# Asking for the weights down one tile at a time in a woven transformer block

## The chip, the cores and the metric

One core of a Trainium2 chip runs the whole kernel. The metric is the time of one execution on the device, in microseconds (us); smaller is better. Engines: PE is TensorE (matmul), PEld its weight loads, ACT ScalarE, DVE VectorE, POOL GpSimd. SP is the sync engine, whose queue (SPq) issues nearly all transfers, in the order in which the program lists them: a request that must wait holds back those behind it.

## What is computed

A transformer block in float32 on 2048 rows of width 512: attention with 32 heads of 16 that share one key and one value head, then a gated feed-forward with 1792 inner columns.

```python
def _A_ref(x, wq, wk, wv, wo):
    q = (x @ wq).reshape(B, S, H, Dh).transpose(0, 2, 1, 3)     # H = 32, Dh = 16
    k, v = x @ wk, x @ wv
    scores = jnp.einsum("bhqd,bkd->bhqk", q, k) * (Dh ** -0.5)
    o = jnp.einsum("bhqk,bkd->bhqd", _softmax(scores), v)
    return o.transpose(0, 2, 1, 3).reshape(B, S, H * Dh) @ wo
def _B_ref(x, w_gate, w_up, w_down):
    return (_gelu(x @ w_gate) * (x @ w_up)) @ w_down
h = x + _A_ref(_layernorm(x), A_wq, A_wk, A_wv, A_wo)
h2 = h + _B_ref(_layernorm(h), B_w_gate, B_w_up, B_w_down)      # the result
```

## The kernel before

Each float32 operand of a dense product is split into a high and a low part (hi, lo), and a product is three matmuls: hi by hi, hi by lo and lo by hi. In the early part of the kernel the split weights are written to DRAM scratch: `w1_d` holds 28 tiles of gate and up weights (512 KB each, gate and up in turn for the 14 column blocks f), and `w2_d` 14 blocks of the weights down, loaded two at a time, so 7 tiles of 1 MB.

The rows are worked in four blocks of 512. Attention of a block goes over 8 groups of four heads. A group has 32 score steps: `scores` makes scores (L362), ACT the exponentials (L366), and `weigh` multiplies by the values (L370). At the end of a group its result leaves to DRAM (`acc_d<-oT`, L384), comes back turned (`oc<-acc_d`, L394), and soon the queries for the next group but one step ahead are asked for (`qg<-q_d`, L347).

The dense part of block b (`dense`) is woven into attention of block b + 1, matmul by matmul, by an order that is written out by hand for PE, ACT, SP and DVE. Only the last block's dense part runs by itself at the end (the tail), with whole matmuls and another order (`solo`, L553).

In the woven dense part 36 products are in a list, the plan: gate and up products (pg, pu), each followed at its end by DVE work (`leave_gate`, `leave_up`), and among them the products down (pd) of two of the four runs in `RUNS`; the products down of the last two runs follow behind the weave (`down`, L531). `weave` runs a product as two halves of 12 matmuls, one on rows 0 to 63 of the array and one on rows 64 to 127, with a lag of 6 steps between a product's halves, three banks, and one matmul in each half of the array per step (L854). When a product's second half is issued, its `done` runs: a gate or up product asks for the tile four further on (`next_w1`, `load_w1`, L511; four buffers). Down tiles (`load_w2`, L516) have three buffers.

Numbered in the order of the plan, products 0 to 11 are gate and up products, 12 to 15 products down (first run), 16 to 23 gate and up, 24 to 27 down (second run), 28 to 35 gate and up. Before, the tiles down are asked for a run at a time: both of the first run at the end of product 3, both of the second at the end of product 15, both of the third at the end of product 27, and the single one of the last run at the end of product 33.

Of the kernel before, what the change touches and what calls it, by code (L numbers as in the profile page):

```python
# [10 lines left out]
F32R = mybir.dt.float32r  # L11
# [8 lines left out]
P = 128  # L20
# [6 lines left out]
PB = 5  # L27

W1 = 4

LAG = 6

# [6 lines left out]
RUNS = ((0, 1, 2, 3), (4, 5, 6, 7), (8, 9, 10, 11), (12, 13))  # L39
# [7 lines left out]
def kernel(  # L47
# [15 lines left out]
    S, D = x.shape  # L63
# [6 lines left out]
    TB = T // P  # L70
    DC = D // P
    FC = F // P
# [76 lines left out]
    def run(outer, first):  # L149
# [8 lines left out]
        width = 0  # L158

        def psum1(name):  # L160
            return ps.tile([P, T], F32, tag="d", bufs=width, name=name)
# [170 lines left out]
        if first:  # L332
            set_banks("ps_pro")
            width = 8
# [109 lines left out]
        db = None  # L444
# [63 lines left out]
        def load_w1(b, i):  # L508

            w = db.tile([P, 2, DC, P], F32R, tag="w1", bufs=W1, name=f"w1_{b}_{i}")  # L510
            nc.sync.dma_start(w.bitcast(F32), w1_d[i].bitcast(F32))  # L511
            return w[:, 0], w[:, 1]

        def load_w2(b, j):
            w = db.tile([P, 2, 2, D], F32R, tag="w2", bufs=3, name=f"w2_{b}_{j}")
            nc.sync.dma_start(  # L516
                w.bitcast(F32), w2_d[2 * j : 2 * j + 2].rearrange("f p i d -> p f i d").bitcast(F32)
            )
            return w[:, :, 0], w[:, :, 1]
# [38 lines left out]
        def dense(b, tail=False):  # L558
# [13 lines left out]
            xT_lo = db.tile([P, DC, T], F32R, tag="x2l", bufs=1, name=f"x2l_{b}")  # L572
            w1 = {i: load_w1(b, i) for i in range(W1)}
            if b == 0:
                yield 0
            w2 = {}
# [134 lines left out]
            def next_w1(i):  # L711
                if i + W1 < 2 * FC:
                    w1[i + W1] = load_w1(b, i + W1)

# [53 lines left out]
                    next_w1(2 * f + k)  # L768
                yield CUT

            def up_plan(f, k, then):
                def terms():
                    hi, lo = w1.pop(2 * f + k)
                    return [
                        (w[:, c, :], xt[:, c, :])
                        for c in range(DC)
                        for w, xt in ((hi, xT_hi), (hi, xT_lo), (lo, xT_hi))
                    ]

                def done(bank):  # L780
                    (leave_up if k else leave_gate)(f, bank)
                    next_w1(2 * f + k)
                    if k:
                        then()

                return f"p{'gu'[k]}_{b}_{f}", terms, done

# [11 lines left out]
            def add_down(t, pd):  # L799
                nc.vector.tensor_tensor(hs[t], hs[t], pd, op=ALU.add)  # L800

            def down_plan(fs, t, tw, then):
                def terms():
                    if t == 0:
                        assert not gates and not lazy or all(j // 2 in gs for j in fs)
                        open_gates()
                        while lazy:
                            lazy.pop(0)()
                        tw.extend(w2.pop(f // 2) for f in fs[::2])
                    return down_terms(fs, tw, t)  # L810

                def done(bank):
                    add_down(t, bank)
                    if t == TB - 1:
                        then()

                return f"pd_{b}_{fs[0]}_{t}", terms, done

            def weave(plan):


                live, ends, jobs = [], {}, [None, None]
                step = opened = 0

                def choose(a):
                    nonlocal opened
                    for e in live:
                        if e["half"] != a and not e["both"] and e["at"] and step >= e["at"] + LAG:
                            e["both"] = True
                            return [e, 0]  # L830
                    free = opened < width or ends.get(opened - width, step) + LAG <= step
                    if opened == len(plan) or not free or a == 1 and step < LAG:
                        return None
                    name, terms, done = plan[opened]
                    e = dict(
                        i=opened, half=a, both=False, at=None, terms=terms(),
                        bank=psum1(name), done=done, name=name,
                    )
                    opened += 1
                    live.append(e)  # L840
                    return [e, 0]

                while opened < len(plan) or live:
                    for a in range(2):
                        if jobs[a] is None:
                            jobs[a] = choose(a)
                    for a in range(2):
                        if jobs[a] is None:
                            continue
                        e, i = jobs[a]  # L850
                        lhsT, rhs = e["terms"][i]
                        rows = slice(64 * a, 64 * a + 64)
                        last = i == len(e["terms"]) - 1
                        nc.tensor.matmul(  # L854
                            e["bank"], lhsT[rows], rhs[rows], start=i == 0 and not e["both"],
                            stop=last and e["both"], skip_group_check=True,
                        )
                        jobs[a][1] += 1
                    step += 1
                    for a in range(2):  # L860
                        if jobs[a] is None or jobs[a][1] < len(jobs[a][0]["terms"]):
                            continue
                        e, jobs[a] = jobs[a][0], None
                        if e["both"]:
                            e["done"](e["bank"])
                            live[:] = [z for z in live if z is not e]
                            ends[e["i"]] = step
                        else:

                            mark = sb.tile(  # L870
                                [P, 1], F32, tag="mark", bufs=3, name=f"mark_{e['name']}"
                            )
                            nc.vector.tensor_copy(mark, e["bank"][:, :1])
                            e["at"] = step
                    yield 1
                yield CUT
# [11 lines left out]
                            nc.sync.dma_start(out_t[:, b * TB + t, :], hs[t])  # L888
                    yield CUT

            def fetch_w2(fs):
                for f in fs[::2]:
                    w2[f // 2] = load_w2(b, f // 2)


            plan, prev = [], None
            for fs in RUNS:
                for n, f in enumerate(fs):
                    then = []
                    if fs is RUNS[-1]:  # L900
                        if n == 0:
                            then.append(fs)
                    elif n == 1 and prev is None:
                        then.append(fs)
                    if tail:
                        yield from up(f)
                        for z in then:
                            fetch_w2(z)
                    else:
                        for k in range(2):  # L910
                            plan.append(up_plan(f, k, partial(
                                lambda zs: [fetch_w2(z) for z in zs], then
                            )))
                    if n != 1 or prev is None:
                        continue
                    if tail:
                        yield from down(prev, False)
                        if fs is not RUNS[-1]:
                            fetch_w2(fs)
                    elif fs is not RUNS[-1]:  # L920
                        tw = []
                        plan.extend(
                            down_plan(prev, t, tw, partial(fetch_w2, fs)) for t in range(TB)
                        )
                prev = fs
            if not tail:
                yield from weave(plan)
                yield from down(RUNS[-2], False)
# [19 lines left out]
        def open_gates():  # L948
            while gates:
                gates.pop(0)()  # L950
# [32 lines left out]
        width = 1  # L983
# [5 lines left out]
        n, lead = 0, 2 * PER + sum(SIZES[: LEAD[0]])  # L989
        with tc.manual_schedule(engines={mybir.EngineType.SP, mybir.EngineType.DVE}):  # L990
# [6 lines left out]
            while n < lead:  # L997
                if n == 2 * PER:
# [5 lines left out]
                    db = late.enter_context(tc.tile_pool(name="dense", bufs=1))  # L1004
# [24 lines left out]
        width = 3  # L1029
# [18 lines left out]
        for c in range(LEAD[0], (NB - 1) * NG * len(SIZES)):  # L1048
            b, cb = divmod(c, NG * len(SIZES))
# [4 lines left out]
            if b > 0 and cb == LEAD[b]:  # L1054
                assert work is None
                work, todo = dense(b), list(kinds)
# [58 lines left out]
        tail = dense(NB - 1, True)  # L1115
# [328 lines left out]
```

## Time and profile before

| | us |
|---|---|
| median of three runs | 1472.63 (1469.05 to 1472.9) |
| the profiled execution, its own time | 1469.96 |
| its span, first to last instruction | 1468.3 |
| PE busy | 1418.2 (97%) |
| ACT busy | 1036.0 (71%) |
| DVE busy | 544.7 (37%) |
| POOL busy | 217.8 (15%) |

The early part lasts to about 310 us. The weave of block 0 lies at about 360 to 603 us, that of block 1 at 684 to 944, that of block 2 at 1031 to 1290; the tail takes the last 120 us. In rows of the profile, a name such as `pg<-x2h,w` means a tile pg written from x2h and a weight tile w; `w` stands for tiles of both kinds, and the line (L511 or L516) tells a request for a gate or up tile from one for a tile down. The granted clock is the share of full speed that TensorE had.

### The profile page before, as it was taken

What the parts mean: (1) busy time and instruction counts of PE and PEld (TensorE: products, weight loads), DVE (VectorE), ACT (ScalarE), POOL (GpSimd) and SP (SyncE); (2) the same over time, 40 slices, a digit from 0 to 9 for tenths busy, and PEclk for the clock granted to TensorE, in tenths of its full rate; (3) what the DMA queues carried; (4) which work ended last, traced back from release to release, by engine and by line L of the source; (5) the groups of instructions that cost most, each with busy time, mean ns of one, the idle gap of its engine ahead of it and who ended that gap; (6) DMA issues with size and microseconds to landing.
All of it is one profiled execution on the core that took longest, in us unless ns stands there. A gap on an engine that the chain in (4) does not pass through costs nothing.

```text
span 1468.3 us, 25088 instructions
## 1 busy us (share of the span) xinstructions
PE 1418.2 (97%) x10420; PEld 761.2 (52%) x10420; DVE 544.7 (37%) x985; ACT 1036.0 (71%) x1145; POOL 217.8 (15%) x301
## 2 busy tenths in 40 slices
PE   6999999999999999999999898999989999899998
PEld 5533333234555555555555454554555455456886
DVE  7422231113342424333432422424252242326665
ACT  6699999996777777777767676777777677672000
POOL 5467766811000000000000000000000000000000
PEclk9999999999999999999999999999999999999999
DMA  4456766741331313131421423212152331344561
GB/s 153 151 188 222 228 224 219 206 148 41 132 122 49 142 63 141 55 135 33 152 78 60 149 70 112 84 63 92 56 169 70 112 109 54 105 139 144 167 217 68
DMA packets 66930, 180.57 MB, mean 123 GB/s; under 512 B 9436, under 2 KB 9436, under 8 KB 66776
## 3 DMA queue, kind: packets, MB, share of 16 engines
q1 hardware_dynamic: 56976, 144.79, 29.4%
q0 software_dynamic: 9760, 34.08, 7.2%
q8 instruction: 84, 1.38, 0.4%
q14 instruction: 38, 0.31, 0.1%
q10 hardware_dynamic: 72, 0.00, 0.0%
HBM read 131.13 MB, written 47.71 MB: 122 GB/s over the span
## 4 chain that ended last, share of the span: by engine, by line
PE 84%; ACT 6%; DMA 5%; DVE 1%; SPq 1%; issue 1%; POOL 0%; ACTq 0%; DVEq 0%
PE acc L370 30%; PE s L362 18%; PE pu L854 8%; PE pg L854 7%; ACT p L366 6%; PE pd L854 5%; DMA w<-w_d 4%; PE pq L188 4%; PE pg L553 3%; PE pd L553 3%; PE pu L553 3%; PE pd L531 2%; PE pp L531 2%; DMA acc_d<-oT 1%; PE pk L1231 1%
## 5 line engine op out<-in xcount | busy, mean ns | idle before, releaser
L366 ACT ACTIVATE p<-s 128x1024 f32<-128x1024 f32 x1024 | 967.0, 1059 | 284.6 <-PE s L362 284.4
L370 PE MATMUL acc<-p,v_sb 128*32 128x512 f32 x4096 | 497.7, 603 | 0.1
L362 PE MATMUL s<-qg,kaug 50*128 50x512 f32 x1984 | 398.8, 434 | 5.4 <-ACT p L366 4.4
L362 PEld LDWEIGHTS s<-qg,kaug 50*128 50x128 f32 x1984 | 174.8, 185 | 286.0 <-ACT p L366 161.2
L854 PE MATMUL pg<-x2h,w 64*128 64x512 f32 x672 | 216.6, 398 | 25.2 <-DMA w<-w_d 25.1
L370 PEld LDWEIGHTS acc<-p,v_sb 128*32 128x32 f32 x4096 | 110.6, 110 | 243.5 <-issue 231.4
L854 PE MATMUL pu<-x2h,w 64*128 64x512 f32 x672 | 217.0, 398 | 0.3 <-DVE g L730 0.3
L124 POOL TENSOR_SCALAR rstd<-mv 128x1 f32<-128x1 f32 x16 | 3.5, 218 | 1027.5 <-DVE mv L122 1027.3
L854 PEld LDWEIGHTS pg<-x2h,w 64*128 64x128 f32 x672 | 118.2, 189 | 40.6 <-issue 26.5
L854 PE MATMUL pg<-x2l,w 64*128 64x512 f32 x336 | 124.5, 399 | 0.0
L854 PEld LDWEIGHTS pu<-x2h,w 64*128 64x128 f32 x672 | 117.7, 188 | 12.1 <-DVE g L730 0.7
L854 PE MATMUL pu<-x2l,w 64*128 64x512 f32 x336 | 124.0, 396 | 0.0
L733 ACT ACTIVATE ga<-ga 128x512 f32<-128x512 f32 x56 | 36.1, 650 | 88.7 <-DVE ga L728 88.7
L854 PE MATMUL pd<-w,gh 64*128 64x512 f32 x384 | 81.5, 391 | 0.0
L1075 DVE SCALAR_TENSOR_TENSOR ga<-ga,g 128x512 f32<-128x512 f32 x72 | 49.8, 691 | 69.6 <-ACT ga L733 68.3
L800 DVE TENSOR_TENSOR h<-h,pd 128x512 f32<-128x512 f32 x48 | 31.8, 684 | 115.7 <-PE pd L854 65.7
L383 DVE COPY oT<-acc 128x512 f32<-128x512 f32 x32 | 22.1, 692 | 141.0 <-PE acc L370 140.9
L399 DVE RECIPROCAL oc<-oc 128x128 f32<-128x128 f32 x64 | 56.3, 921 | 29.2 <-DMA oc<-acc_d 26.5
L717 DVE COPY g<-pg 128x512 f32<-128x512 f32 x56 | 38.7, 691 | 65.3 <-PE pg L854 59.6
L854 PEld LDWEIGHTS pu<-x2l,w 64*128 64x128 f32 x336 | 58.9, 188 | 6.1
L854 PEld LDWEIGHTS pg<-x2l,w 64*128 64x128 f32 x336 | 59.1, 189 | 5.4
L730 DVE TENSOR_TENSOR g<-g,pu 128x512 f32<-128x512 f32 x56 | 38.3, 683 | 40.4 <-PE pu L854 30.4
(251 smaller groups left out, 1386.0 us busy)
## 6 DMA issues: line engine op xcount, KB each, us to landing
w<-w_d SPq DMA_DIRECT2D x112, 512.0 KB
w<-w_d SPq DMA_DIRECT2D x28, 1024.0 KB
qg<-q_d SPq DMA_DIRECT2D x62, 200.0 KB
q_d<-qh SPq DMA_DIRECT2D x32, 256.0 KB
acc_d<-oT SPq DMA_DIRECT2D x32, 256.0 KB
oc<-acc_d SPq DMA_DIRECT2D x128, 64.0 KB
w_d<-w_0b POOLq DMA_DIRECT2D x14, 512.0 KB, 6.3
w_d<-w_1b POOLq DMA_DIRECT2D x14, 512.0 KB, 3.8
```

Of the source, the lines that this page charges most:

```text
L188: nc.tensor.matmul(pq, wt[:, d, c * P : (c + 1) * P], xt[:, d, :], start=(n == 0), stop=(n == 3 * DC - 1),)
L362: nc.tensor.matmul(s[:, a, :], kaug[rows, kc * P : (kc + 1) * P], qg[rows, u, :], start=True, stop=True,)
L366: nc.scalar.activation(p[:, 2 * u : 2 * u + 2, :], s, AF.Exp, scale=SCALE)
L370: nc.tensor.matmul(acc[32 * j : 32 * j + 32, :], v_sb[:, kc, :], p[:, j, :], start=(kc == 0), stop=(kc == KC - 1), skip_group_check=True,)
L399: nc.vector.reciprocal(oc[:, 1, sl], oc[:, 1, sl])
L531: nc.tensor.matmul(banks[k], lhsT[rows], rhs[rows], start=(turn == 0 and i == 0), stop=(turn == 1 and i == n - 1), skip_group_check=True,)
L553: nc.tensor.matmul(bank, lhsT, rhs, start=(i == 0), stop=(i == len(ts) - 1))
L717: nc.vector.tensor_copy(g, pg)
L730: nc.vector.tensor_tensor(g, g, pu, op=ALU.mult)
L733: nc.scalar.activation(a, a, AF.Tanh, scale=GELU_A * GELU_C)
L854: nc.tensor.matmul(e["bank"], lhsT[rows], rhs[rows], start=i == 0 and not e["both"], stop=last and e["both"], skip_group_check=True,)
L1075: (soon or lazy).pop(0)()
```

## The change

Requests for tiles down no longer hang on the products' own `done` (the `then` arguments go). Instead `weave` asks for one tile after the end of every third product (numbers 2, 5, 8 and so on), if there is a tile left (7 per block) and a buffer is free by count: `over` counts tiles whose run of products down has ended, and tile g is asked for only when g is below `over` plus 3. Tile size, buffers, products and their order stay. In the tail the requests stand where they stood, written in another way.

```diff
+W2 = 3
...
-            def up_plan(f, k, then):
+            def up_plan(f, k):
...
                     next_w1(2 * f + k)
-                    if k:
-                        then()
...
-            def down_plan(fs, t, tw, then):
+            def down_plan(fs, t, tw):
...
                 def done(bank):
+                    nonlocal over
                     add_down(t, bank)
                     if t == TB - 1:
-                        then()
+                        over += len(tw)
...
+            over = 0
...
                         if e["both"]:
                             e["done"](e["bank"])
+
+                            g = max(w2, default=over - 1) + 1
+                            if e["i"] % width == width - 1 and g < FC // 2 and g < over + W2:
+                                w2[g] = load_w2(b, g)
...
-            def fetch_w2(fs):
-                for f in fs[::2]:
-                    w2[f // 2] = load_w2(b, f // 2)
...
-                            plan.append(up_plan(f, k, partial(
-                                lambda zs: [fetch_w2(z) for z in zs], then
-                            )))
...
+                        plan.extend(up_plan(f, k) for k in range(2))
...
-                            down_plan(prev, t, tw, partial(fetch_w2, fs)) for t in range(TB)
+                        plan.extend(down_plan(prev, t, tw) for t in range(TB))
```

More of the change, by code (lines that the diff above doesn't have):

```diff
@@ L514, in load_w2 @@
         def load_w2(b, j):
-            w = db.tile([P, 2, 2, D], F32R, tag="w2", bufs=3, name=f"w2_{b}_{j}")
+            w = db.tile([P, 2, 2, D], F32R, tag="w2", bufs=W2, name=f"w2_{b}_{j}")
             nc.sync.dma_start(
@@ L898, in dense @@
                 for n, f in enumerate(fs):
[L899 to L904, printed above, removed]
                     if tail:
                         yield from up(f)
-                        for z in then:
-                            fetch_w2(z)
-                    else:
-                        for k in range(2):
-                            plan.append(up_plan(f, k, partial(
-                                lambda zs: [fetch_w2(z) for z in zs], then
-                            )))
-                    if n != 1 or prev is None:
-                        continue
-                    if tail:
+                    else:
+                        plan.extend(up_plan(f, k) for k in range(2))
+                    if tail and fs is RUNS[-1] and n == 0:
+                        w2[f // 2] = load_w2(b, f // 2)
+                    if tail and n == 1 and prev is not None:
                         yield from down(prev, False)
-                        if fs is not RUNS[-1]:
-                            fetch_w2(fs)
-                    elif fs is not RUNS[-1]:
+                    if tail and n == 1 and fs is not RUNS[-1]:
+                        for g in fs[::2]:
+                            w2[g // 2] = load_w2(b, g // 2)
+                    if not tail and n == 1 and prev is not None and fs is not RUNS[-1]:
                         tw = []
-                        plan.extend(
-                            down_plan(prev, t, tw, partial(fetch_w2, fs)) for t in range(TB)
-                        )
+                        plan.extend(down_plan(prev, t, tw) for t in range(TB))
                 prev = fs
```

## The prediction

> **What bounds the kernel now.** I read the head of the page first, then the list of who waited for whom, then the stretches of time between two heads, and last the sync engine's own timeline at the places where TensorE waits.
>
> ```profile
> span 1468.3 us, 25088 instructions
> PE 1418.2 (97%) x10420; PEld 761.2 (52%) x10420; DVE 544.7 (37%) x985; ACT 1036.0 (71%) x1145; POOL 217.8 (15%) x301
> ...
> L854 PE MATMUL pg<-x2h,w 64*128 64x512 f32 x672 | 216.6, 398 | 25.2 <-DMA w<-w_d 25.1
> ...
> w<-w_d SPq DMA_DIRECT2D x112, 512.0 KB
> w<-w_d SPq DMA_DIRECT2D x28, 1024.0 KB
> ```
>
> TensorE (PE) is busy for 97% of the span, so time comes off only where it works less, works faster or does not wait. L854 is the matmul of the weave. Of all its idle time, 25.1 us are spent waiting for a weight tile (w<-w_d). The other engines (ACT 71%, DVE 37%) have room.
>
> ```profile
> PE pg L854 <- DMA w<-w_d: 25.1, 7, 4.7
> ...
> PE pg L854 <- DMA w<-w_d: 0.9, 1, 0.9
> ...
> PE pg L854 <- DMA w<-w_d: 4.7, 1, 4.7
> ...
> PE pg L854 <- DMA w<-w_d: 3.8, 1, 3.8
> ...
> PE pg L854 <- DMA w<-w_d: 4.0, 1, 4.0
> ```
>
> The columns are us in total, times, longest. The first row is the whole span: seven waits. The others are single stretches: block 0 (0.9), and the three of block 1 (4.7, 3.8, 4.0). Block 2 has the three that are left, 25.1 - 0.9 - 12.5 = 11.7 us. All are before a gate product (pg), so what is late is a tile of the gate and up weights (512 KB), not a tile of the weights down.
>
> What does such a wait cost in the end? I cut the span at the moments when a group of four heads ends (the sync engine's transfer acc_d<-oT, L384). Between two of these lies the same work, 342 matmuls. The columns: stretch, length, PE, PEld, DVE, ACT and POOL busy, granted clock, DMA share, GB/s.
>
> ```profile
> 429.91:470.39 40.48, 40.48 (x342) 22.09 (x340) 10.60 (x21) 31.09 (x35) 0.00 (x0) 1.00 0.20 63
> 470.39:510.89 40.50, 40.50 (x342) 22.18 (x340) 18.21 (x32) 31.09 (x35) 0.00 (x0) 1.00 0.42 141
> 551.37:593.10 41.73, 40.78 (x342) 22.23 (x340) 18.33 (x32) 31.20 (x35) 0.00 (x0) 1.00 0.34 124
> 717.90:765.59 47.69, 42.77 (x342) 24.22 (x340) 20.22 (x36) 31.99 (x36) 0.00 (x0) 0.96 0.38 131
> 806.10:852.10 46.00, 42.24 (x342) 22.50 (x340) 18.34 (x32) 31.20 (x35) 0.00 (x0) 0.96 0.37 124
> 892.56:940.14 47.58, 43.55 (x342) 23.32 (x340) 18.29 (x32) 31.30 (x35) 0.00 (x0) 0.93 0.31 109
> ...
> 1064.70:1111.01 46.31, 42.39 (x342) 23.89 (x340) 20.22 (x36) 31.99 (x36) 0.00 (x0) 0.96 0.40 134
> 1151.52:1198.74 47.22, 43.63 (x342) 22.68 (x340) 18.38 (x32) 31.20 (x35) 0.00 (x0) 0.93 0.34 121
> 1239.21:1285.71 46.50, 42.34 (x342) 23.02 (x340) 18.28 (x32) 31.30 (x35) 0.00 (x0) 0.96 0.35 123
> ```
>
> A stretch without a wait takes 40.48 us with TensorE busy throughout. The second row also holds two tiles of the weights down (141 GB/s) and takes 40.50, so the transfers themselves cost nothing; being waited for does. The seven with a wait are longer by 1.25, 7.21, 5.52, 7.10, 5.83, 6.74 and 6.02 us: 39.7 us. That is more than the 25.1 us of waiting, and the granted clock says why: 0.96 or 0.93 in the six long ones, 1.00 in the one with 0.9 us.
>
> ```profile
> 569.00:571.00 2.00, 2.00 (x20) 0.42 (x16) 0.08 (x1) 1.88 (x3) 0.00 (x0) 1.00 0.00 0
> ...
> 738.00:740.00 2.00, 2.00 (x12) 1.77 (x12) 0.28 (x2) 0.70 (x1) 0.00 (x0) 0.50 0.00 0
> ```
>
> Behind the wait of 0.9 us the clock stays at 1.00 (20 matmuls in 2 us); behind that of 4.7 us it is at 0.50 (12 matmuls). One minus the clock, times the length, summed over the six stretches: 1.91 + 1.84 + 3.33 + 1.85 + 3.31 + 1.86 = 14.1 us. With 25.1 us of waiting that is 39.2, nearly the 39.7 found from the lengths. I use 39.7.
>
> The Trainium skill ("TensorE: Matmul & The Clock Gate", Part 1) says that an idle window of about 3.4 us halves the clock and that about 3.4 us of work restores it. By that alone each of the six waits would cost one window at half speed, 1.7 us, and all seven 25.1 + 10.2 = 35.3 us. The trace agrees with the halving (0.50) but not with one window each: 0.93 over 47.58 us is twice that.
>
> **Why the tile is late.** The sync engine's requests (SPq) around one of the waits, then the vector engine's instructions there, then rows of the chain of waits for the three heads of block 1:
>
> ```profile
> 806.10 0.32 SPq L384 DMA_DIRECT2D acc_d<-oT  x1
> 808.19 1.72 SPq L394 DMA_DIRECT2D oc<-acc_d  x4
> 809.95 0.94 SPq L516 DMA_DIRECT2D w<-w_d  x2
> 810.99 0.41 SPq L511 DMA_DIRECT2D w<-w_d  x1
> 811.45 1.06 SPq L347 DMA_DIRECT2D qg<-q_d  x2
> ```
>
> ```profile
> 807.19 0.69 DVE L800 TENSOR_TENSOR h<-h,pd 128x512 f32<-128x512 f32 x1 [1.11 <-PE pd L854]
> 809.13 0.69 DVE L717 COPY g<-pg 128x512 f32<-128x512 f32 x1 [1.25 <-PE pg L854]
> ```
>
> ```profile
> 725.37 11.17 DMA w<-w_d
> ...
> 810.99 8.03 DMA w<-w_d
> ...
> 897.46 7.61 DMA w<-w_d
> ```
>
> Number the weave's products 0 to 35. Three are in flight. The plan's arithmetic (12 steps to a half, a lag of 6, three banks) makes them end in threes: 3j, 3j+1 and 3j+2 end 6 steps apart, then 24 steps pass. At 807.19 the fourth product of the first run down ends (number 15), and its end asks for two down tiles, 2 MB (L516). At 809.13 the gate product 16 ends, and the gate tile that it asks for (L511, 810.99) stands behind those 2 MB. It lands 8.03 us later, and product 20, which opens 12 steps after 16 ends, waits for it. The pairs behind products 3 and 27 do the same to the tiles for products 8 and 32. The end that asks for two down tiles is each time the first of its three, and the next end, 6 steps later, asks for the tile with the short deadline.
>
> **The change, part by part.**
>
> *The requests down.* They stay seven per block of the same 1 MB, and the buffers stay three, so no instruction, byte or memory is added. They go behind the last end of a three: by the two conditions, behind products 2, 5, 8, 17, 20, 29 and 32. None waits for its buffer: tile 3 takes that of tile 0, whose last reader, product 15, is over two ends earlier; tiles 5 and 6 take those of 2 and 3, read up to product 27. So nothing queues behind a waiting request. None is late: products 12 and 24 and the two products down behind the weave use tiles asked for at the latest behind products 5, 20, 29 and 32.
>
> *What the gate tile then finds in the queue.* Nothing but what stood there already. How long does one take alone?
>
> ```profile
> 839.12 0.32 SPq L511 DMA_DIRECT2D w<-w_d  x1
> ```
>
> ```profile
> 840.00:841.00 1.00, 1.00 (x12) 0.76 (x10) 0.97 (x2) 1.00 (x3) 0.00 (x0) 1.00 0.89 279
> 841.00:842.00 1.00, 1.00 (x12) 0.39 (x12) 0.94 (x3) 1.00 (x3) 0.00 (x0) 1.00 0.72 262
> ```
>
> Asked for at 839.12, its bytes (541 KB in the two rows) have moved by 842: 2.9 us. At 806 the request moves up to 809.95, so it lands at about 812.9; TensorE began to wait at 810.99 + 8.03 + 0.14 - 3.8 = 815.4 (0.14 us is the gap from landing to matmul: 0.9 of wait and its first matmul at 567.59 against the landing at 567.46). Margin 2.5 us. At 892 the same sum, 1.03 us earlier than 897.46, gives 899.3 against 901.2: 1.9 us. Block 2 repeats this. The first head of a block is the tightest: there another gate tile and the queries (qg, 400 KB) stand in front.
>
> ```profile
> 722.06 1.38 SPq L511 DMA_DIRECT2D w<-w_d  x1
> 723.48 0.95 SPq L516 DMA_DIRECT2D w<-w_d  x2
> 724.47 0.80 SPq L347 DMA_DIRECT2D qg<-q_d  x2
> ```
>
> Without the two L516 requests the tile is asked for at about 725.37 - 0.95 = 724.4. Two gate tiles and the queries are 1.46 MB, 5.4 us at the 270 GB/s above; with data flowing from about 724.4 it lands at 729.8 if later requests do not slow it. If all that is asked for behind it (another gate tile, one down tile, 1.57 MB) mixed evenly with it, 5.8 us more: 735.6. TensorE waits from 725.37 + 11.17 + 0.14 - 4.7 = 732.0. I take 729.8, since the ends of requests follow their order in the rows, and keep 735.6 for a rival.
>
> *What the down tile does to the next gate tile.* The ends behind which it now stands are followed by the long gap:
>
> ```profile
> 484.52 0.34 SPq L511 DMA_DIRECT2D w<-w_d  x1
> 497.71 0.32 SPq L511 DMA_DIRECT2D w<-w_d  x1
> ```
>
> Product 17's request and product 18's are 13.2 us apart where nothing stalls. A down tile is two gate tiles' bytes, some 5 us at 270 GB/s. It is done when the next gate tile is asked for. Cost: nothing, covered by the weave's own work; if the cover went, the second rival but one gives the price.
>
> *The last block.* It keeps its order of requests down (it does not go through the weave), so I cost it at nothing. Up to 2 us either way could come if its requests are ordered differently among themselves; nothing in the rows shows that.
>
> *Sum.* Seven stretches return to 40.48 us: -39.7 us. The profiled execution took 1469.96 us (its span and 1.7 us around it); that gives 1430.3. The median of the three runs is 1472.63, 2.7 us above it; that gives 1432.9. Stretches without waits agree within 0.05 us, so much of the difference between runs probably sits in the waits, which go. I say 1431.
>
> **The rivals.**
>
> *The first heads still wait* (chance 0.13). The tile for product 8 lands near 735.6 as above, 3.6 us late, in blocks 1 and 2. Then 7.21 + 5.83 = 13.0 us stay: 1444. For it: a margin of 2 us with 1.57 MB asked for right behind. Against it: two of the later requests come when most of its bytes have moved.
>
> *Only one clock window a wait is to be had* (0.05). By the page's rule above the gain would be 35.3 us: 1435. Against it: the lengths of the stretches, which need no theory of the clock.
>
> *The gate tile is late without the down tiles* (0.05). If the transfers at the end of a head (256 KB to acc_d, 256 KB back, the queries) made it late, the change would gain nothing: 1470. For it: every wait lies behind such an end. Against it: 429.91 to 470.39 has the same end and no down tiles, and no wait.
>
> *The down tile delays the next three* (0.04, the other side). Four of the seven places per block (behind 2, 5, 17 and 29) are followed by a gate tile with a deadline. If a down tile took longer than those 13.2 us and some 3 us of slack, each would cost what a stretch lost before, 38.4/6 = 6.4 us: 12 x 6.4 = 77 us, so 1431 + 77 = 1508. It decides from about 16 us for 1 MB; 2 MB and a gate tile took 8.03 us above, so it is far off.
>
> **How the numbers follow.** All seven waits gone has 0.70 (own range 1427 to 1437). The others have the chances given; 0.03 is left for causes unnamed. The range 1426 to 1446 takes in the first two rivals and leaves out 0.12 and some of the tails. Measurement tells about 0.3% (4 us) from no change. Faster: 0.70 + 0.13 + 0.05 + 0.02 = 0.90; same 0.05 (the third rival); slower 0.05 (the fourth and a remainder).
>
> **What would show it.** Right: the group "PE pg L854 <- DMA w<-w_d" is gone from the list of waits or under 2 us; the 24 whole stretches of the weave all take about 40.5 us; the granted clock is 1.00 up to the last block; the sync engine's L516 requests come singly, some 20 us apart. Wrong: waits left at the first head of blocks 1 and 2; waits of TensorE for w at products 7, 10, 22 or 34, which would be new; L516 requests that wait for a matmul; or a longer last block.

## The result, and the profile after

| | before | after |
|---|---|---|
| median, us | 1472.77 (four runs, 1469.05 to 1473.31) | 1431.58 (four runs, 1430.93 to 1433.07) |
| profiled execution, us | 1469.96 | 1430.93 |
| its span, us | 1468.3 | 1429.2 |

The ratio is 0.9727, with a 95% interval of 0.9709 to 0.9745: 2.7% faster. The forecast was 1431.

First the head of the page and two of its groups; L858 is the matmul of the weave, L854 before.

```profile
span 1429.2 us, 25063 instructions
...
PE 1403.6 (98%) x10420; PEld 754.8 (53%) x10420; DVE 543.8 (38%) x985; ACT 1034.3 (72%) x1145; POOL 218.1 (15%) x301
...
L858 PE MATMUL pu<-x2h,w 64*128 64x512 f32 x672 | 211.7, 392 | 0.5 <-DMA w<-w_d 0.4
L858 PE MATMUL pg<-x2h,w 64*128 64x512 f32 x672 | 211.2, 391 | 0.0
```

As many matmuls as before, 10420. The gate products' idle time of 25.2 us is 0.0, and their matmuls take 391 ns on the mean instead of 398, since none runs at half clock. One wait of 0.4 us for a weight tile is left, before an up product (pu).

Now the stretches between the ends of two heads, cut as before. These stand for the seven that had a wait (block 0: one, block 1: three, block 2: three).

```profile
550.88:591.29 40.41, 40.41 (x342) 22.09 (x340) 18.34 (x32) 31.05 (x35) 0.00 (x0) 1.00 0.37 129
...
716.16:757.16 41.00, 40.90 (x342) 22.45 (x340) 20.23 (x36) 31.77 (x36) 0.00 (x0) 1.00 0.45 152
797.64:838.05 40.41, 40.41 (x342) 22.05 (x340) 18.44 (x32) 31.06 (x35) 0.00 (x0) 1.00 0.40 141
878.52:918.99 40.47, 40.47 (x342) 22.11 (x340) 18.29 (x32) 31.08 (x35) 0.00 (x0) 1.00 0.39 128
...
1043.52:1084.75 41.23, 40.87 (x342) 22.45 (x340) 20.21 (x36) 31.76 (x36) 0.00 (x0) 1.00 0.46 151
1125.25:1165.69 40.44, 40.44 (x342) 22.11 (x340) 18.34 (x32) 31.07 (x35) 0.00 (x0) 1.00 0.42 141
1206.15:1246.65 40.50, 40.50 (x342) 22.14 (x340) 18.29 (x32) 31.08 (x35) 0.00 (x0) 1.00 0.43 141
```

Their lengths were 41.73, 47.69, 46.00, 47.58, 46.31, 47.22 and 46.50, and the granted clock (the number after POOL) was 0.93 to 0.96 in six of them. It is 1.00 now. Added up, the seven became 38.6 us shorter, of the 39.1 us by which the span fell.

The sync engine's requests at the place that the prediction showed (then 806 to 814):

```profile
797.64 0.32 SPq L386 DMA_DIRECT2D acc_d<-oT  x1
799.68 1.72 SPq L396 DMA_DIRECT2D oc<-acc_d  x4
801.50 0.37 SPq L513 DMA_DIRECT2D w<-w_d  x1
801.91 0.76 SPq L349 DMA_DIRECT2D qg<-q_d  x2
805.06 0.35 SPq L513 DMA_DIRECT2D w<-w_d  x1
805.46 0.43 SPq L518 DMA_DIRECT2D w<-w_d  x1
```

The gate tile (L513) follows the head's return (oc) directly. The down tile (L518), now a single one, comes last, behind the third end.

### The profile page after: what moved, and what is told of

The parts are those of the page before. It is cut to its first block, busy times and chain, and to the rows that moved or that the text cites. A ratio compares the mean times of both kernels' runs of the same rounds, so it can differ in the third digit from the quotient of the medians.

```text
span 1429.2 us, 25063 instructions
## 1 busy us (share of the span) xinstructions
PE 1403.6 (98%) x10420; PEld 754.8 (53%) x10420; DVE 543.8 (38%) x985; ACT 1034.3 (72%) x1145; POOL 218.1 (15%) x301
## 4 chain that ended last, share of the span: by engine, by line
PE 89%; ACT 6%; DVE 2%; issue 1%; DMA 1%; POOL 0%; SPq 0%; ACTq 0%; DVEq 0%; POOLq 0%
PE acc L372 31%; PE s L364 19%; PE pu L858 9%; PE pg L858 7%; ACT p L368 6%; PE pd L858 5%; PE pq L190 3%; PE pg L555 3%; PE pd L555 3%; PE pu L555 3%; PE pd L533 2%; PE pp L533 2%; PE pxt L608 1%; PE pk L1223 0%; DMA w<-w_d 0%
## 5 line engine op out<-in xcount | busy, mean ns | idle before, releaser
L372 PE MATMUL acc<-p,v_sb 128*32 128x512 f32 x4096 | 492.4, 598 | 0.1
L858 PE MATMUL pu<-x2h,w 64*128 64x512 f32 x672 | 211.7, 392 | 0.5 <-DMA w<-w_d 0.4
L858 PE MATMUL pg<-x2h,w 64*128 64x512 f32 x672 | 211.2, 391 | 0.0
L858 PEld LDWEIGHTS pu<-x2h,w 64*128 64x128 f32 x672 | 116.0, 186 | 13.2 <-DVE g L732 0.8
L858 PE MATMUL pg<-x2l,w 64*128 64x512 f32 x336 | 122.4, 392 | 0.0
L858 PEld LDWEIGHTS pg<-x2h,w 64*128 64x128 f32 x672 | 116.1, 186 | 11.7
L858 PE MATMUL pu<-x2l,w 64*128 64x512 f32 x336 | 122.2, 391 | 0.0
L858 PE MATMUL pd<-w,gh 64*128 64x512 f32 x384 | 81.8, 391 | 0.0
L858 PEld LDWEIGHTS pu<-x2l,w 64*128 64x128 f32 x336 | 58.0, 186 | 6.8
L858 PEld LDWEIGHTS pg<-x2l,w 64*128 64x128 f32 x336 | 58.0, 186 | 5.1
```

The source lines that it names most:

```text
L372: nc.tensor.matmul(acc[32 * j : 32 * j + 32, :], v_sb[:, kc, :], p[:, j, :], start=(kc == 0), stop=(kc == KC - 1), skip_group_check=True,)
L858: nc.tensor.matmul(e["bank"], lhsT[rows], rhs[rows], start=i == 0 and not e["both"], stop=last and e["both"], skip_group_check=True,)
```

## The experiments

Three theories stood against each other. A: the place decides; a down tile must not be asked for ahead of a gate tile with a short deadline. B: one tile at a time is what helps. C: the bytes at the end of a head hurt, wherever they stand in the queue. An end is that of a product in its three, as in the prediction; the second column gives the place in the program. Each ratio is to the kernel before, timed beside the run.

| run | down tiles | us | ratio to before (95%) |
|---|---|---|---|
| e1 | pairs, one end later | 1432.8 | 0.9738 (0.9719 to 0.9757) |
| e2 | pairs, third end | 1431.6 | 0.9727 (0.9708 to 0.9746) |
| e3 | single, first end | 1445.89 | 0.9823 (0.9803 to 0.9844) |
| e12 | single, second end | 1433.44 | 0.9737 (0.972 to 0.9753) |
| e4 | pairs, first end, GpSimd's queue | 1448.3 | 0.9852 (0.9827 to 0.9877) |
| e5 | e4, reciprocals later | 1438.88 | 0.9778 (0.9761 to 0.9794) |
| e6 | pairs, third end, GpSimd's queue | 1446.59 | 0.9828 (0.9805 to 0.9851) |
| e9 | pairs, first end, ScalarE's queue | 1476.31 | 1.0031 (1.0017 to 1.0046) |
| e10 | pairs, third end, ScalarE's queue | 1433.26 | 0.9743 (0.9724 to 0.9761) |
| e7 | single, third end, loaded twice | 1437.93 | 0.9769 (0.9753 to 0.9785) |
| e8 | single, third end, loaded three times | 1453.05 | 0.9866 (0.9848 to 0.9883) |
| e11 | changed kernel, reciprocals later | 1431.56 | 0.9726 (0.971 to 0.9742) |

### Place or number: e1, e2, e3, e12

All four replace the rule in `weave` by a table of ends and tiles:

```diff
-                            g = max(w2, default=over - 1) + 1
-                            if e["i"] % width == width - 1 and g < FC // 2 and g < over + W2:
+                            for g in ASKS.get(e["i"], ()):
                                 w2[g] = load_w2(b, g)
+ASKS = {4: (0, 1), 16: (2, 3), 28: (4, 5), 33: (6,)}                           # e1
+ASKS = {5: (0, 1), 17: (2, 3), 29: (4, 5), 32: (6,)}                           # e2
+ASKS = {0: (0,), 3: (1,), 6: (2,), 15: (3,), 18: (4,), 27: (5,), 30: (6,)}     # e3
+ASKS = {1: (0,), 4: (1,), 7: (2,), 16: (3,), 19: (4,), 28: (5,), 31: (6,)}     # e12
```

> The kernel before, but each pair of down tiles is asked for one end later: behind products 4, 16 and 28 instead of 3, 15 and 27 (still two tiles at once, still at the end of a head). Theory, order in the queue: the gate tile with the short deadline (for products 8, 20, 32) is now asked for just ahead of the 2 MB, so its wait goes: 1431 to 1436 us, TensorE waits for w under 3 us in all, clock 0.99 or more. Rival, the amount at the end of a head is what hurts: 2 MB are still asked for there, so the waits stay near 25 us and the time is 1460 to 1473 us.

> Down tiles asked for at the changed kernel's kind of place (the last end of a three) but in pairs: behind 5, 17 and 29, and the single one behind 32. Theory, the place decides: the long gap of some 13 us behind these ends covers 2 MB as well, 1431 to 1434 us. Rival, one tile at a time is what matters: the gate tile asked for next lands late by about 1 MB (some 3 us) at products 7, 19 or 31 or their neighbours, and the time is 1440 to 1455 us.

> One tile at a time, but behind the first end of a three (products 0, 3, 6, 15, 18, 27, 30), where the pairs stood before. Theory, order in the queue: 1 MB stands in front of the gate tile instead of 2 MB, so it lands some 2.5 us sooner than before: of 3.6 to 4.7 us of wait 1 to 2 us stay at each end of a head in blocks 1 and 2, in all 5 to 12 us, too short to halve the clock (0.99 or more): 1436 to 1445 us. If the clock is halved behind short waits too: 1445 to 1455 us. Rival, one tile at a time is enough wherever it stands: 1431 to 1434 us.

> One tile at a time behind the second end of a three (products 1, 4, 7, 16, 19, 28, 31), which completes the row with e3 (first end) and the changed kernel (third end). Theory, what is asked for first is served first: the request now comes right behind that of the gate tile with the short deadline, so nothing waits for it: 1431 to 1434 us, waits of TensorE for w under 2 us. Rival, sharing: the down tile takes part of the engines' time from the gate tile asked for just ahead of it, whose margin is 2 us: waits at products 8, 20 and 32 of 1 us or so, 1435 to 1442 us.

The waits for w, from the list of who waited for whom. In e1 and e12 that group is gone; the first fence is e2's. The second is e3's, first the whole span, then three single stretches, and the third has those stretches' own rows in the same order (2.4, 1.8 and 1.9 us of wait):

```profile
PE pu L860 <- DMA w<-w_d: 0.7, 2, 0.5
```

```profile
PE pg L860 <- DMA w<-w_d: 10.0, 6, 2.4
PE pg L860 <- DMA w<-w_d: 2.4, 1, 2.4
PE pg L860 <- DMA w<-w_d: 1.8, 1, 1.8
PE pg L860 <- DMA w<-w_d: 1.9, 1, 1.9
```

```profile
716.50:761.83 45.33, 42.72 (x342) 24.27 (x340) 20.21 (x36) 32.03 (x36) 0.00 (x0) 0.96 0.39 138
884.35:927.47 43.12, 41.04 (x342) 22.43 (x340) 18.29 (x32) 31.46 (x35) 0.00 (x0) 1.00 0.35 120
1135.04:1179.35 44.31, 42.37 (x342) 22.43 (x340) 18.48 (x32) 31.19 (x35) 0.00 (x0) 0.96 0.38 129
```

Pairs at the third end (e2) are as fast as single tiles there, so B falls: at that place the change's "a tile at a time" does nothing for the time. Single tiles at the second end (e12) give 1433.44 without a wait for w, so the rival of sharing (1435 to 1442) falls too. Moving the pairs by a single end, from the first to the second (e1), is enough for 38 us (from 1471.23, the median of before in those runs, to 1432.8). Its requests at the same head show how little that is:

```profile
802.10 0.37 SPq L515 DMA_DIRECT2D w<-w_d  x1
802.51 0.94 SPq L520 DMA_DIRECT2D w<-w_d  x2
```

The pair (L520) is still asked for there, 0.4 us behind the gate tile (L515) instead of 1 us ahead, and nothing waits. So C in its simple form falls too. Single tiles at the first end (e3) leave waits of 0.9 to 2.4 us, as 1 MB in front instead of 2 should; of the three places tried, only here does the number count. The time, at 1445.89, is just above what I gave for an unhalved clock, because behind two of the six waits it was halved.

### Another queue: e4, e5, e6, e9, e10

```diff
-            nc.sync.dma_start(                                        # load_w2
+            (nc.gpsimd if b < NB - 1 else nc.sync).dma_start(         # e4 (places as before), e6 (as e2)
+            (nc.scalar if b < NB - 1 else nc.sync).dma_start(         # e9 (places as before), e10 (as e2)
```

> The kernel before with its pairs at their old places, but in blocks 0 to 2 they are asked for by GpSimd on its own queue; the gate and up tiles stay on the sync engine's. Theory, order in one queue: the gate tile no longer stands behind the pair; it shares the engines with it and lands some 2 us after it would alone: at most 1 us of wait at each place, 1431 to 1438 us. Rival, the bytes in flight decide whatever the queue: waits as before, 1460 to 1473 us.

> Pairs asked for by GpSimd on its own queue, but at the place of e2, behind products 5, 17 and 29 (the single one behind 32). Theory, the place decides: behind these ends the head's round trip is over and no tile with a short deadline is asked for, so the queue does not matter: 1431 to 1435 us. Rival, GpSimd's queue itself costs (its requests, or its share of the engines): 1440 to 1450 us as in e4.

I expected e4 to settle whether standing behind the pair in one queue is what counts. Neither side came out (1448.3), and e6 was no better than e4 though it has e2's places. GpSimd's own rows, e4 first, then e6:

```profile
796.94 0.72 POOL L516 DMA_DIRECT2D w<-w_d  x1 [117.31 <-PE pd L854]
801.93 0.72 POOL L516 DMA_DIRECT2D w<-w_d  x1 [4.27 <-PE s L362]
```

```profile
798.29 0.71 POOL L520 DMA_DIRECT2D w<-w_d  x1 [117.83 <-PE pu L860]
803.25 0.71 POOL L520 DMA_DIRECT2D w<-w_d  x1 [4.25 <-PE pd L860]
```

Both ask at the same moments (the stretches end 1.3 us apart, at 800.58 and 801.91). GpSimd had been idle for 117 us and issued a request as soon as its semaphores let it, here the first of the pair ahead of the head's end. On the sync engine the place in the program is kept because the requests ahead in the queue wait for the ends of their products (in the kernel before, L511 waits 141.9 us in all for gate products); on this idle queue it meant nothing. So e6 did not test what it was built for, and its time, in the range of its rival, says nothing for that rival. What e4 shows is another wait. The sync engine's requests, VectorE's wait and TensorE's in it:

```profile
800.58 0.32 SPq L384 DMA_DIRECT2D acc_d<-oT  x1
805.13 1.82 SPq L394 DMA_DIRECT2D oc<-acc_d  x4
```

```profile
DVE oc L399 <- DMA oc<-acc_d: 4.1, 1, 4.1
```

```profile
PE pg L854 <- DVE mark_pg L873: 8.4, 4, 2.3
PE pg L854 <- DMA w<-w_d: 1.5, 1, 1.5
```

From acc_d to oc it takes 4.55 us instead of the usual 2.1, because the pair went out ahead. VectorE stands in front of its reciprocals (L399) until oc lands, so it comes late to the mark (a copy of one column behind a product's first half, `mark_pg`), and TensorE waits for that. e5 moves the reciprocals away:

```diff
-                outs.extend([[] for _ in range(4 if b == 0 else 1)])
+                outs.extend([[] for _ in range(4 if b == 0 else 2 if g < NG - 1 else 1)])
```

> The same as e4 (pairs at their old places, asked for by GpSimd), but the reciprocals of a pair of heads (L399) come one stretch of six score steps later in the order of VectorE. In e4 the pair went out ahead of the head's round trip through DRAM and made it slower (acc_d 4.5 instead of 2.0 us, oc 3.3 instead of 1.9 us). Theory, a second path: the waits left in e4 are those of a bank that VectorE frees late because it sits in front of the reciprocals until oc lands; with these later, the waits under the vector engine's name (8.4 us) go: 1431 to 1438 us. Rival, the gate tile itself is late when it shares the engines with the pair: the waits stay, now under the transfer's name, 1443 to 1450 us.

```profile
PE pg L854 <- DMA w<-w_d: 4.9, 6, 1.2
PE pu L854 <- DMA w<-w_d: 0.7, 1, 0.7
```

The waits for the mark go (no wait for VectorE is left in the weave), the time falls by 9.4 us, to 0.9 us above the range given, and 5.6 us of waiting for weight tiles come up. So the second path is shown, and the first lies close behind it (no wait over 1.2 us). ScalarE's queue, where the exponentials around a request hold its place in the program, was to make the test that e4 missed:

> The kernel before with its pairs at their old places, but in blocks 0 to 2 they are asked for on ScalarE's queue. Unlike GpSimd's queue in e4 and e6, which went ahead of its place as soon as the buffers were free, ScalarE's is held to its place by the exponentials around the requests. So the pair comes after the head's round trip was asked for, as before, but not in the same queue as the gate tile. Theory, order in one queue: the gate tile has only a share of the engines to lose, half the 2.6 us or so that its 512 KB take, and some for the queries: at most 1.5 us of wait at each place, no halved clock at most of them, 1431 to 1442 us. Rival, the bytes in flight decide: waits of 3 to 4 us stay, 1455 to 1473 us. A held ScalarE (waiting for the last reader of a buffer) would show as TensorE waiting for p.

> ScalarE's queue at the place of e2 (pairs behind 5, 17 and 29, the single one behind 32). Theory, the place decides and this queue keeps it: 1431 to 1436 us, where GpSimd's queue at the same place in the program gave 1446.6 us because it did not keep it. Rival, a second queue is what cost there: 1440 to 1450 us.

e9 did not keep the old place in time either. On the sync engine the pair goes out behind oc's requests, 3.85 us behind acc_d (806.10 and 809.95 before); on ScalarE's queue it went out ahead of oc. e9's requests in order of time, both queues, and VectorE's wait (its row names w, the semaphore that came last by the profile; what the reciprocals read is oc, whose last request landed at 818.41, by the last of its 16 completion counts in the trace):

```profile
806.75 0.32 SPq L384 DMA_DIRECT2D acc_d<-oT  x1
807.01 0.92 ACTq L516 DMA_DIRECT2D w<-w_d  x2
809.89 1.96 SPq L394 DMA_DIRECT2D oc<-acc_d  x4
811.95 0.37 SPq L511 DMA_DIRECT2D w<-w_d  x1
```

```profile
818.73 1.76 DVE L399 RECIPROCAL oc<-oc 128x128 f32<-128x128 f32 x2 [6.80 <-DMA w<-w_d]
```

```profile
PE pg L854 <- DVE mark_pg L873: 18.8, 4, 5.0
PE pu L854 <- DMA w<-w_d: 11.1, 2, 5.8
```

So a pair behind oc in a queue of its own stays untested. What e9 shows is that a queue of its own does not take the pair out of the way, and in that form the theory of one queue falls. By the completion counts oc's four requests took 6.7 to 7.5 us to land here, instead of 2.3 to 2.5, and the gate tile 8.0 us, as before. TensorE waits 18.8 us for VectorE and 12.5 us for weight tiles, and 1476.31 us is above even the rival's range. e10, with the same queue at the third end, gives 1433.26, as expected. So the place in time decides, on either queue: theory A holds, in that form.

### How wide is the cover: e7, e8

```diff
+            for _ in range(1 if b < NB - 1 else 0):        # e7; range(2 ...) in e8; in load_w2
+                nc.sync.dma_start(w.bitcast(F32), w2_d[2 * j : 2 * j + 2].rearrange("f p i d -> p f i d").bitcast(F32))
```

> The changed kernel, but in blocks 0 to 2 each down tile is loaded twice in a row into the same buffer, the second request waiting on the sync engine until the first has landed: 2 MB and a held queue per place. How wide is the cover? Theory: two loads in a row take some 11 us, under the 13.2 us to the next gate tile's request, so nothing waits: 1431 to 1436 us. Rival, the cover is thinner than its 13.2 us (the next gate tiles or the head's round trip suffer): 1440 us or more.

> The same with three loads in a row, some 16 us, which is more than the 13.2 us. Theory: the next gate tile stands behind the third load, and the round trip of the next head too; at the four places of seven that are followed by a gate tile with a short deadline, and at heads' ends, waits of 1 to 4 us come back: 1440 to 1480 us. Rival, slack is larger than thought: under 1436 us.

e7's first long stretch (350 matmuls instead of 342, since acc_d, at which it is cut, goes out late), a later one, and the sync engine around the start of the first (L518 the down tile, L522 its second load):

```profile
389.83:437.69 47.86, 44.58 (x350) 23.49 (x350) 20.11 (x38) 32.82 (x37) 0.00 (x0) 0.93 0.53 174
844.37:884.85 40.48, 40.48 (x342) 22.13 (x340) 10.59 (x21) 31.08 (x35) 0.00 (x0) 1.00 0.20 63
```

```profile
383.89 0.43 SPq L518 DMA_DIRECT2D w<-w_d  x1
389.37 0.37 SPq L522 DMA_DIRECT2D w<-w_d  x1
389.83 0.41 SPq L386 DMA_DIRECT2D acc_d<-oT  x1
395.62 1.73 SPq L396 DMA_DIRECT2D oc<-acc_d  x4
```

A down tile takes 5.5 us from request to landing (the second load waited for that). Two in a row cost nothing at 20 of the 21 places. At the first place of block 0 the head ends only 5 us later (acc_d goes out at 388.92 in the changed kernel). The second load holds acc_d up (to 389.83, and then 5.8 us to oc instead of 2.1), VectorE waits 6.8 us for oc, and TensorE 3.3 us for VectorE: the second path again. That one place gives all of the loss, and my 1431 to 1436 missed by 2 us. Three in a row are too much, 1453.05, within the range given; its longest waits are 8.1 us for VectorE and 3.7 us for a tile.

### What is left: e11

> The changed kernel with the reciprocals one stretch of score steps later (the edit of e5). If the 0.5 to 0.8 us that the first whole stretch of blocks 1 and 2 still has over 40.48 us come from VectorE in front of the reciprocals, they go: 1429 to 1431 us, which the measurement can hardly tell from the changed kernel's 1431.6. If not, 1431 to 1433 us.

1431.56: no difference. In e11's profile the first whole stretches of blocks 1 and 2 still take 41.39 and 41.18 us, so the reciprocals are not the reason for what they have over 40.48. It stays open, and it is worth 1.3 us in all in the changed kernel. No version beats the changed kernel; e2 equals it.

## Why the prediction was right

*The price of the waits.* The step that used lengths of stretches and not the listed waits held: 39.7 us forecast, 39.1 off the span. The seven stretches gave 38.6 of it; the first heads of blocks 1 and 2 stay 0.5 and 0.8 us over 40.48. The 25.1 us of waits alone would have given 1446. The estimate by the rule of the Trainium skill ("TensorE: Matmul & The Clock Gate", Part 1) was 35.3 us, which the result does not bear out; the last section shows why two of the waits cost two windows. The step from span to median held as well: the profiled execution was 2.8 us below the median before and is 0.65 below it now.

*The deadlines.* The margins of the gate tile were enough: no wait at products 8, 20 or 32. They were thinner than forecast, though. By the completion counts the tile took 3.5 to 4.0 us to land at the four later heads, not 2.9; 2.5 us was forecast as left at the first of these and 1.9 at the second, 1.9 and 0.5 were. At the first heads I had forecast the tile for product 8 at 11.9 us behind acc_d, with 14.1 as the limit; it landed at 12.9 (block 1) and 11.7 (block 2). The rival's end, 735.6 by even mixing with later requests, is 17.7 on that scale. e1 refutes it: with 2 MB right behind, the tile landed at 13.4 and 12.1.

*Not foreseen, but small.* The 0.4 us that is left is at product 7 of block 2. I had listed a new wait at product 7 as a sign against the forecast. Its tile is asked for right behind the head's return, as before, and took 4.7 us to land. That fits the rival of the traffic at the head's end, to which I gave 0.05, but no run shows it; e1, e11 and e12 do not have the wait.

*Half right.* "Stands behind those 2 MB" in the queue: e9 loses as much with the pair in another queue, where it was asked for ahead of oc. What e1 and e12 show to be the cause is the order of the requests in time; one queue is how the kernel before came to that order.

*Missed.* The cover. I counted 13.2 us to the next gate tile and named a limit of 16 us, and did not look at the head's round trip, which is a second path to TensorE through VectorE. At the first place of block 0 the head ends 5 us behind the down tile's request, so the tile (5.5 us) is still landing when acc_d goes out. The change pays nothing for it (388.92 to 429.44 takes 40.52 us), but twice the bytes did.

*Slips of the text.* Product 24 uses tiles asked for behind products 8 and 17; the list in the prediction leaves these out. The stretches of 342 matmuls in the weave are five per block, 15, not 24. The requests for tiles down come singly, but 15 to 60 us apart, not some 20 throughout.

## What to carry to other kernels

Price a late transfer by the length of the stretch around it against the same stretch without a wait, not by the wait alone: behind it the clock may be halved. When a tile is late, look for what was asked for just ahead of it in time, on any queue, and move that behind the next request with a deadline; here one place in the order was worth 38 us, and behind that place the number of tiles asked for at once nothing. Before moving bulk traffic into a gap, list every round trip that ends in the gap, not only the transfer that was late.

## What the runs showed of the hardware

Waits shorter than those of the kernel before also halved the clock, but not all of them: in e3 behind 1.9 and 2.4 us, not behind 0.9, 1.4, 1.7 and 1.8. The Trainium skill ("TensorE: Matmul & The Clock Gate", Part 1) has it that an idle window of about 3.4 us halves the clock; these runs differ, and the measurement decides. In e4 a wait of 2.2 us left it at 1.00, and one of 2.1 us did not (the two waits, then windows of 3.41 us there):

```profile
PE pg L854 <- DVE mark_pg L873: 2.2, 1, 2.2
PE pg L854 <- DVE mark_pg L873: 2.1, 1, 2.1
```

```profile
892.29:895.70 3.41, 2.23 (x20) 1.36 (x16) 1.32 (x2) 2.86 (x3) 0.00 (x0) 1.00 1.03 269
895.70:899.11 3.41, 2.37 (x20) 1.34 (x24) 1.05 (x3) 1.58 (x2) 0.00 (x0) 1.00 0.71 178
899.11:902.52 3.41, 3.41 (x32) 1.62 (x26) 1.33 (x4) 1.87 (x3) 0.00 (x0) 1.00 0.00 0
...
1226.80:1230.21 3.41, 1.27 (x12) 1.05 (x12) 2.17 (x4) 1.31 (x2) 0.00 (x0) 1.00 0.89 207
1230.21:1233.62 3.41, 3.41 (x20) 0.79 (x20) 1.02 (x2) 2.10 (x3) 0.00 (x0) 0.50 0.14 55
```

The windows are not chosen freely: in each trace the moments at which the granted clock changes lie whole multiples of 3.41 us apart. The wait of 2.2 us fell on two such windows (idle 1.18 and 1.04 us), that of 2.1 us on one. Cut in this way, the 14 traces agree without exception. Before the end of the work each of the 21 windows at full clock with 1.75 us or more of TensorE's idling, about half a window, was followed by half clock, and none with 1.68 us or less was. A window at half clock was followed by full clock where it held at most 0.46 us of idling, and by another at half clock from 0.62 us on. So in the kernel before the waits of 3.6 and 4.0 us, which reached 0.62 and 0.84 us into the next window, cost two windows each, and that of 4.7 us one.

A transfer asked for behind the pair on the other hardware queue began late. In e9's packet records the sync engine's queue moved nothing from 809.0 to 813.0 us, while ScalarE's pair did, though oc had been asked for at 809.89 (on a free queue its bytes follow some 0.8 us behind the request). Once both had begun, they took turns: from 897.0 to 898.5 us, at another head, acc_d moved 101 packets of 2 KB and the pair 101 of 4 KB. So what was asked for first had the start, but not the engines to itself. What holds the start back is not shown.
